# A bias table on POOL's DMA queue, block weights on VectorE, and a longer POOL list at the start of a fused attention and expert kernel

## The chip, the cores and the metric

The kernel runs as one program on one core of a Trainium2 chip. The metric is the device time of one execution in microseconds (us). Before the change the median of three runs is 571.19 us (570.97 to 571.46).

## The reference

Attention with a learned relative bias, then a token and channel mixer, then eight experts of which each token takes one. Only the first part is touched by the change:

```python
B, H, S, D = q.shape                      # 2, 8, 576, 64
scores = scale * np.matmul(q, k.transpose(0, 1, 3, 2))
psi_rel = np.log1p(np.abs(rel))
psi_i = np.log1p(np.maximum(pos[:, None].astype(np.float32), 1.0))
x = (psi_rel / psi_i)[..., None]
h = np.maximum(x @ w1 + b1, 0.0)          # 576 x 576 x 32
bias = h @ w2                             # 576 x 576 x 8
scores = scores + bias.transpose(2, 0, 1)[None, :, :, :]
```

The softmax of the scores, the product with `v`, the mixer and the experts follow.

## The kernel before

The bias is a two-layer network over all pairs of positions, made once per query tile and shared by both batches. It is made in 36 groups of 16 query rows. In one group, 128 partitions hold 4 rows times 32 hidden units, and four parts of 576 columns make 16 rows. The first layer of a group is `bias_hidden` (L484 to L498): each part is one instruction of 128x576, the relu of a table times a scale, on VectorE, POOL (`eng.tensor_scalar`, L497) or ScalarE (L494). It needs the table `tabs`, the scale `sc` and `negb`, the negative of the table `b1c` (`bias_setup`, L463 to L465). The second layer is `bias_mm` (L500): eight matmuls against `wblk`, a 128x32 matrix with the 32x8 weights `w2r` four times on its block diagonal (L196, L197). ScalarE adds a constant `cb` and moves the result out as `ev` (L510), and SP's queue spreads it into the tile's bias (L516 or L518). There are two buffers for a group's first layer, so the first layer of group n+2 waits for the matmuls of group n.

Four of the groups belong to the last query tile, the tail, which is worked first. Before the loop over steps there is a start of hand-written order: `load_const` (L174) issues the loads of the tables and of the first keys and queries, lets TensorE multiply zeros, and builds `wblk`; then `ORDER["start"]` (L58) lists what is emitted on all engines. In that list `hidden0` to `hidden5` and `bias0` to `bias4` are the two layers of the groups, `const` makes `cb` with small matmuls against `wblk` (L479, L481), `zero` clears the query buffers `qt` on POOL (L297, L298), `tail_split` splits the tail's queries in two precisions (`qm`, on POOL, L203 and L305), and `key_T` and `key_split` transpose and split keys (`kn` to `K`; L269, L203, L282). Each engine works off its instructions in this order, and waits by semaphores alone. Which engine takes a part of a first layer is a string in `ENGINE` (L65): the n-th group takes the n-th letter, counted round, so that `start1="VVP"` gives the second part of groups 0 to 4 to V, V, P, V, V (V is VectorE, P is POOL, A is ScalarE).

After the start comes one step per pair of heads and query tile: scores on TensorE (L370), bias and row maximum on VectorE (L348), exponential on ScalarE (L351), and so on. The mixer and the experts are not touched.

Of the kernel before, what the change touches and what calls it, by code (L numbers as in the profile page):

```python
# [54 lines left out]
QO = 3, 3, 3, 6  # L55

ORDER = {
    "start": "hidden0 const load_k2 tail_split0 hidden1 bias0 hidden2 bias1 key_T00 hidden3 zero key_T01 key_T11 key_T10 key_split0 tail_split1 bias2 hidden4 bias3 load_k4 hidden5 key_split1 tail_T bias4 load_v load_q".split(),  # L58
    "first": "scores0 hidden2 last_T prob_T0 values key_T0 normalize query_T tail_T query_split hidden1 hidden0 key_T1 bias_mm key_split out_T tail_split hidden3 query_rest".split(),
    "mixed": "hidden2 scores0 values tail_T query_T normalize hidden0 last_T prob_T0 key_T0 key_T1 query_split tail_split hidden1 key_split bias_mm query_rest out_T hidden3".split(),  # L60
    "bias": "query_T query_split hidden3 scores0 scores1 last_T values hidden0 query_rest hidden2 late bias_mm out_T mix prob_T0 prob_T1 hidden1 normalize".split(),
    "edge": "hidden0 bias_mm mix hidden2 last_T hidden3 prob_T0 scores0 scores1 values query_T prob_T1 normalize query_split query_rest late hidden1 out_T".split(),
    "plain": "scores0 last_T query_T scores1 values normalize prob_T0 prob_T1 out_T query_split query_rest late mix".split(),
}
ENGINE = dict(key0="A", key1="A", keyl0="V", keyl1="A", qlo="P", mhi="P", mlo="P", qhi="AP", qT="A", qT0="V", qT1="AVV", prob0="A", prob1="AV", last="V", half0="V", half1="A", xlo="PPPPVPPVV", val="V", val0="V", hidden0="V", hidden1="VP", hidden2="PV", hidden3="A", early0="V", early1="A", early2="P", early3="A", start0="VA", start1="VVP", start2="V", start3="VA")  # L65

LATE = dict(alloc_mix=9, decode=[10, 12, 14, 16, 17, 20, 22, 24, 26], split_wt2=[-3, -4, 0, -4, 8, 21, 23, 25, 28], split_wt1=[33, 34, 37, 36, 36], split_x=[32, 34, 36, 37, 38, 37, 38, 39])
GATE = -1.7881393e-07
# [40 lines left out]
def body(ctx, tc, q, k, v, w1, b1, w2, wt1, wt2, wc1, wc2, wg, wl, mw1, mw2,  # L109
# [17 lines left out]
    with tc.manual_schedule():  # L127
        tok = ctx.enter_context(ExitStack())
        mix = TokenMix(nc, x)
        attention(tc, nc, tok, mix, q, k, v, w1, b1, w2, c_L, c_id, ident, x, wt1, wt2, prefill)  # L130
        if "x" in dbg:
            nc.sync.dma_start(dbg["x"], x)
        R = Routing(tc, nc, wg, wl, ident, c_tok, c_small, x2d, meta)
        X = Experts(tc, nc, R, Rings(tc, ctx, "big", side="right"), x_p, mw1, mw2, ident, x2d, meta, out)
        mixer(tc, nc, tok, mix, wc1, wc2, ident, x, R, X)
        if "x2" in dbg:
            nc.sync.dma_start(dbg["x2"], x2d)
        X.rest()
        X.close()
        R.close()  # L140


def attention(tc, nc, tok, mix, q, k, v, w1, b1, w2, c_L, c_id, ident, x, wt1, wt2, prefill):
# [10 lines left out]
    with ExitStack() as ctx:  # L154
# [8 lines left out]
        def alloc_ps():  # L163
            return ps_t.tile([128, 512], F32, name="tp", tag="tr")
# [4 lines left out]
        b1c = cst.tile([128, 1], F32, name="b1c")  # L169
        w2r = cst.tile([128, H], F32, name="w2r")  # L170
        wblk = cst.tile([128, 32], F32, name="wblk")

        def load_const():
            four = lambda ap, n: ap.rearrange("(a k) o -> a k o", a=1).to_broadcast([4, HID, n])  # L174

            cut = 4 * NG + S + 128
            warm = cst.tile([128, 1], F32, name="warm")
            nc.vector.memset(warm, 0.0)
            nc.scalar.activation(warm, warm, AF.Exp)
            nc.sync.dma_start(tabs[:, 0:cut], c_L[:, 0:cut])  # L180
            nc.scalar.dma_start(w1c, four(w1.rearrange("o k -> k o"), 1))
            nc.sync.dma_start(b1c, four(b1.rearrange("(k o) -> k o", o=1), 1))
            nc.sync.dma_start(w2r, four(w2, H))
            load_k(0)
            load_q(*steps[0])
            nc.sync.dma_start(tabs[:, cut:], c_L[:, cut:])
            nc.sync.dma_start(ident, c_id)

            zero = x[:, 0]
            nc.vector.memset(zero, 0.0)  # L190
            ps = alloc_ps()
            for _ in range(WARM):
                nc.tensor.matmul(ps, lhsT=zero[:, 0:128], rhs=zero, start=True, stop=True)
            nc.gpsimd.memset(wblk, 0.0)
            for ii in range(4):
                r = slice(32 * ii, 32 * ii + 32)  # L196
                nc.gpsimd.tensor_copy(wblk[r, 8 * ii:8 * ii + 8], w2r[r])  # L197

        turns = {what: cycle(engines) for what, engines in ENGINE.items()}

# [19 lines left out]
        def load_k(i):  # L220

            b, pr = divmod(i, NP)
            n = nat_p.tile([128, 20, D], F32, name="kn", tag="kn", bufs=2)
            main, hs = n[:, 0:16].rearrange("p (n h) d -> p n h d", h=4), k[b, 2 * pr:2 * pr + 4]
            for j in range(NIT):
                nc.sync.dma_start(main[:, j], hs[:, 128 * j:128 * j + 128].rearrange("h p d -> p h d"))
            nc.sync.dma_start(n[0:64, 16:20], hs[:, 512:S].rearrange("h p d -> p h d"))
            for j in range(2):
                nat["k", i + j] = main[:, :, 2 * j:2 * j + 2], n[0:64, 16 + 2 * j:18 + 2 * j]
# [14 lines left out]
        def load_q(it, i):  # L244

            b, pr = divmod(i, NP)
            n = nat_p.tile([128, 4, D], F32, name="qn", tag="qn", bufs=2)
            if it == NIT:
                tv = q[b, :, 512:S].rearrange("(a e) p d -> e p a d", e=2)
                for e in range(2):  # L250
                    nc.sync.dma_start(n[64 * e:64 * e + 64], tv[e])
                for j in range(NP):
                    nat["q", it, i + j] = n[:, j]
            else:
                nc.sync.dma_start(n, q[b, 2 * pr:2 * pr + 4, 128 * it:128 * it + 128].rearrange("h p d -> p h d"))
                nat["q", it, i] = n
# [210 lines left out]
        def hidden_by(g):  # L467

            n = groups.index(g)
            phase = "start" if n < ahead else "early" if n < ahead + B * NP else "hidden"  # L470
            return "".join(e[n % len(e)] for e in (ENGINE[f"{phase}{qq}"] for qq in range(4)))

# [114 lines left out]
        def split_x(n):  # L587
# [3 lines left out]
            else:  # L591
                hl = [kv_p.tile([128, DM], F32R, name="xs", tag=f"K{n - (n > LAST)}{a}") for a in range(2)]
            nc.scalar.copy(hl[0], x[:, n])
            (nc.gpsimd if ENGINE["xlo"][n] == "P" else nc.vector).tensor_tensor(
                hl[1], x[:, n], hl[0].bitcast(F32), ALU.subtract)
# [32 lines left out]
        def late_fetch(s):  # L628

            if pieces and any(f is decode for f, *_ in late.get(s, ())):  # L630
                fetch(pieces.pop(0))

        load_const()
        bias_setup()
        start = {
            "const": (bias_const,), "zero": (query_zero,), "load_k2": (load_k, 2), "load_k4": (load_k, 4), "load_v": (load_v, 0),
            "load_q": (load_q, *steps[NP]), "tail_T": (tail_T, *steps[0]),
        }
        for n in range(2):
# [691 lines left out]
class Experts:  # L1331
# [93 lines left out]
    def weights(self, t, a):  # L1425
        nc, tab = self.nc, self.R.tab
        if t not in self.sel:
            self.sel[t] = (nc.values_load(tab[0:1, 1, t:t + 1], engines=[SP], min_val=0, max_val=E - 1),
                           nc.values_load(tab[0:1, 2, t:t + 1], engines=[SP], min_val=0, max_val=1))
        e, changed = self.sel[t]  # L1430
        self.load(a, e, **(dict(cond=changed) if t > NSAME else {}))
# [359 lines left out]
```

## Time and profile before

| | us |
|---|---|
| median of three runs | 571.19 (570.97 to 571.46) |
| the profiled execution, its own time | 572.25 |
| its span in the trace | 570.1 |
| busy: TensorE, VectorE, ScalarE, POOL | 543.3, 381.8, 331.9, 244.3 |

The profiled execution takes 2.15 us more than its span, and lies 1.06 us above the median of the runs. Times in the trace count from the start of the span. A row of a timeline has the start, the time to the end of the last of its instructions, the engine, the line, the operation, what it writes and reads, how many instructions were merged, and in brackets how long the engine was idle before it and what ended that. Merged instructions of one engine overlap a little, since one starts before the one ahead has written its last value.

### The profile page before, as it was taken

How to read it: one execution, taken by the hardware profiler on the slowest of the kernel's cores; microseconds unless marked ns; L12 is line 12 of the kernel's file. 1: busy time of each engine (PE TensorE's matmuls, PEld its weight loads, DVE VectorE, ACT ScalarE, POOL GpSimd, SP SyncE). 2: the span in 40 equal slices, each digit the busy share in tenths (PEclk: the TensorE clock that was granted, in tenths of full speed). 3: DMA queues.
4: the chain of work that ended last, by engine and by line, in shares of the span. 5: the costliest groups of instructions: out<-in, count | busy, mean ns of one | idle time of the engine just before them, and what ended most of it. 6: DMA issues, size and time to landing. Idle time of an engine off the chain costs nothing.

```text
span 570.1 us, 11965 instructions
## 1 busy us (share of the span) xinstructions
PE 543.3 (95%) x4306; PEld 428.7 (75%) x4306; DVE 381.8 (67%) x886; ACT 331.9 (58%) x622; POOL 244.3 (43%) x236
## 2 busy tenths in 40 slices
PE   8799899999999999999999989999999999999992
PEld 3466677777778977789999867787778778786871
DVE  6788798989987764898888247533681235669640
ACT  5799799899897862444444133123323357776760
POOL 4787656566772540244444102300033145647541
PEclk9999999999999999999999999999999999999997
DMA  6794875765654430344441030270004973566950
GB/s 166 176 199 111 187 172 145 174 148 128 162 131 114 121 102 2 111 121 147 152 161 55 0 93 1 83 268 20 19 20 139 392 272 121 188 251 209 363 168 13
DMA packets 72417, 79.92 MB, mean 140 GB/s; under 512 B 37127, under 2 KB 51725, under 8 KB 72349
## 3 DMA queue, kind: packets, MB, share of 16 engines
q1 hardware_dynamic: 68924, 73.80, 45.0%
q0 software_dynamic: 2176, 5.26, 2.7%
q8 instruction: 36, 0.59, 0.5%
q14 instruction: 33, 0.26, 0.1%
q10 hardware_dynamic: 1248, 0.01, 0.1%
HBM read 72.08 MB, written 5.34 MB: 136 GB/s over the span
## 4 chain that ended last, share of the span: by engine, by line
PE 68%; DVE 12%; ACT 7%; issue 6%; DMA 4%; POOL 1%; SPq 0%; POOLq 0%; ACTq 0%; DVEq 0%
PE ph L770 20%; PE po L770 15%; PE tp L436 5%; PE py L770 5%; PE ps L507 5%; PE ps L370 4%; PE tp L421 3%; ACT t L351 2%; DMA bias<-ev 2%; DVE t L348 2%; DVE K L282 2%; PE tp L770 1%; PE tp L1476 1%; DVE raw L754 1%; DMA raw<-in_moe_w_ch_dram 1%
## 5 line engine op out<-in xcount | busy, mean ns | idle before, releaser
L497 POOL TENSOR_SCALAR hd<-tabs,sc,negb 128x576 f32<-128x576 f32 x32 | 76.6, 2395 | 3.3 <-PE tp L452 1.8
L770 PE MATMUL po<-cw,h 128*128 128x512 f32 x272 | 67.3, 395 | 0.0
L351 ACT ACTIVATE t<-t,st 128x576 f32<-128x576 f32 x72 | 55.4, 770 | 18.4 <-DVE st L348 18.3
L1439 DVE TENSOR_TENSOR big<-raw,big 128x1024 fp32r<-128x1024 f32 x30 | 43.8, 1485 | 21.9 <-ACT big L1438 21.7
L770 PEld LDWEIGHTS po<-cw,h 128*128 128x128 f32 x272 | 49.8, 188 | 10.0 <-issue 0.4
L348 DVE CUSTOM_DVE_ANT_0 t<-ps,bias 128x576 f32<-128x576 f32 x72 | 52.2, 750 | 7.2 <-PE ps L370 4.5
L370 PE MATMUL ps<-K,qt 128*128 128x288 f32 x320 | 54.0, 309 | 2.8 <-DVE qt L209 2.0
L436 PE MATMUL tp<-pt,v 128*64 128x128 f32 (+1 forms) x800 | 49.3, 268 | 0.0
L1217 POOL DMA_INDIRECT meta<-tokid,posi x10 | 10.0, 996 | 90.3 <-DVE tokid L1214 54.4
L370 PEld LDWEIGHTS ps<-K,qt 128*128 128x128 f32 x320 | 44.5, 189 | 5.2 <-POOL t L362 2.1
L770 PE MATMUL py<-big,hT 128*128 128x512 f32 x184 | 47.9, 400 | 0.1
L507 PE MATMUL ps<-hd,wblk 128*32 128x288 f32 x576 | 45.2, 418 | 2.3 <-DVE st L348 1.1
L1438 ACT CAST big<-raw 128x1024 fp32r<-128x1024 f32 x44 | 44.2, 1055 | 2.7 <-DMA big<-in_moe_w_dram 1.0
L436 PEld LDWEIGHTS tp<-pt,v 128*64 128x64 f32 x800 | 40.2, 137 | 7.4 <-issue 5.3
L770 PE MATMUL ph<-big,xT 128*128 128x512 f32 x168 | 43.2, 404 | 1.1 <-DVE xT L1453 1.1
L497 DVE TENSOR_SCALAR hd<-tabs,sc,negb 128x576 f32<-128x576 f32 x69 | 41.8, 636 | 0.1
L762 POOL TENSOR_TENSOR big<-wf,big 128x512 fp32r<-128x512 f32 x12 | 18.7, 1558 | 51.1 <-ACT big L761 51.1
L770 PEld LDWEIGHTS py<-big,hT 128*128 128x128 f32 x184 | 33.8, 188 | 8.2 <-issue 0.6
L494 ACT ACTIVATE hd<-tabs,b1c,sc 128x576 f32<-128x576 f32 x43 | 36.9, 866 | 3.9 <-DVE sc L465 3.8
L1439 POOL TENSOR_TENSOR big<-raw,big 128x1024 fp32r<-128x1024 f32 x10 | 27.5, 2750 | 24.9 <-ACT big L1438 24.9
L770 PEld LDWEIGHTS ph<-big,xT 128*128 128x128 f32 x168 | 30.5, 189 | 10.0 <-issue 1.6
L421 PE MATMUL tp<-ident,t 128*128 128x128 f32 x256 | 34.2, 275 | 0.0
(304 smaller groups left out, 1189.1 us busy)
## 6 DMA issues: line engine op xcount, KB each, us to landing
raw<-in_moe_w_dram SPq DMA_DIRECT2D x48, 512.0 KB
raw<-in_moe_w_ch_dram SPq DMA_DIRECT2D x24, 512.0 KB
bias<-ev SPq DMA_DIRECT2D x32, 288.0 KB
qt<-qs SPq DMA_DIRECT2D x64, 128.0 KB
lw<-in_moe_w_dram SPq DMA_DIRECT2D x16, 512.0 KB
big<-in_moe_w_dram SPq DMA_DIRECT2D x8, 512.0 KB
lw<-in_moe_w_dram SPq DMA_DIRECT2D x16, 256.0 KB
big<-in_moe_w_dram SPq DMA_DIRECT2D x16, 256.0 KB
```

What stands on the lines that cost most here:

```text
L348: nc.vector.tensor_tensor_reduce(t.rearrange("p (a j) -> p a j", a=2), ps[:, :, 0:HALF], bs.rearrange("p (a j) -> p a j", a=2), op0=ALU.ad ...
L351: nc.scalar.activation(t, t, AF.Exp, bias=st[:, j:j + 1], scale=-1.0, accum_out=st[:, 2 + j:3 + j])
L370: nc.tensor.matmul(ps[:, hf, 0:HALF], lhsT=qt[:, j], rhs=K[k][:, hf * HALF:(hf + 1) * HALF], start=j == pairs[0][0], stop=j == pairs[-1][0])
L421: nc.tensor.transpose(tp[:, 128 * j:128 * j + 128], tt[:, o:o + 128], ident)
L436: nc.tensor.matmul(po[64 * h:64 * h + 64, 0:rhs.shape[1]], lhsT=lhsT, rhs=rhs, start=j == 0, stop=j == 4)
L494: nc.scalar.activation(hd[:, qq], Lt[:, o:o + S], AF.Relu, bias=b1c, scale=sc[:, c])
L497: eng.tensor_scalar(hd[:, qq], Lt[:, o:o + S], sc[:, c], negb, ALU.mult, ALU.max)
L507: nc.tensor.matmul(ps[32 * qq:32 * qq + 32, hf, 0:HALF], lhsT=wblk, rhs=hd[:, qq, hf * HALF:(hf + 1) * HALF], start=True, stop=True)
L762: nc.gpsimd.tensor_tensor(lo, src, hi.bitcast(F32), ALU.subtract)
L770: nc.tensor.matmul(out, lhsT=lhs[a], rhs=rhs[b], start=first and i == 0, stop=last and i == 2)
L1438: nc.scalar.copy(hi, raw)
L1439: (nc.gpsimd if c == 3 and t else nc.vector).tensor_tensor(lo, raw, hi.bitcast(F32), ALU.subtract)
```

## The change

Four edits, all at the start. The load of `b1c` is issued on POOL's queue instead of SP's. The four copies that build `wblk` leave `load_const` for a function of their own, run on VectorE, and stand behind `hidden0` in the list. The clearing of the query buffers goes from the middle of the list to its head. And `ENGINE` has `start1="VPPVVP"` where it had `start1="VVP"`, which for the five groups means V, P, P, V, V instead of V, V, P, V, V: one part of `hidden1` goes from VectorE to POOL.

```diff
 ORDER = {
-    "start": "hidden0 const load_k2 tail_split0 hidden1 bias0 hidden2 bias1 key_T00 hidden3 zero key_T01 key_T11 key_T10 key_split0 tail_split1 bias2 hidden4 bias3 load_k4 hidden5 key_split1 tail_T bias4 load_v load_q".split(),
+    "start": "zero hidden0 weights hidden1 const load_k2 tail_split0 bias0 hidden2 bias1 key_T00 hidden3 key_T01 key_T11 key_T10 key_split0 tail_split1 bias2 hidden4 bias3 load_k4 hidden5 key_split1 tail_T bias4 load_v load_q".split(),
...
-            nc.sync.dma_start(b1c, four(b1.rearrange("(k o) -> k o", o=1), 1))
+            nc.gpsimd.dma_start(b1c, four(b1.rearrange("(k o) -> k o", o=1), 1))
             nc.sync.dma_start(w2r, four(w2, H))
...
             nc.gpsimd.memset(wblk, 0.0)
+
+        def weights():
             for ii in range(4):
                 r = slice(32 * ii, 32 * ii + 32)
-                nc.gpsimd.tensor_copy(wblk[r, 8 * ii:8 * ii + 8], w2r[r])
+                nc.vector.tensor_copy(wblk[r, 8 * ii:8 * ii + 8], w2r[r])
...
-            "const": (bias_const,), "zero": (query_zero,), "load_k2": (load_k, 2), "load_k4": (load_k, 4), "load_v": (load_v, 0),
+            "const": (bias_const,), "weights": (weights,), "zero": (query_zero,), "load_k2": (load_k, 2), "load_k4": (load_k, 4), "load_v": (load_v, 0),
```

Lines behind the new function are two higher in the changed kernel (L497 becomes L499). TensorE's and ScalarE's instructions keep their order; SP's list loses one load, its second. The two other lists change as follows.

POOL, from the start of the program's own instructions to the second `qm` pair; before:

```order
L194 MEMSET wblk_103 128x32
L197 COPY wblk_103<-w2r_102 32x8 x4
L203 CAST qm_177<-qn_121 128x2x64
L305 ISA
L305 TENSOR_TENSOR qm_177<-qn_121,qm_177 128x64
L497 TENSOR_SCALAR hd_199<-tabs_99,sc_107,negb_106 128x576
L297 MEMSET qt0_104 128x2x2x64
L298 MEMSET qt0_104 128x2x2x64
L297 MEMSET qt1_105 128x2x2x64
L298 MEMSET qt1_105 128x2x2x64
L203 CAST qm_256<-qn_121 128x2x64
```

The same place on POOL now:

```order
L182 DMA b1c_101<-in_b1_dram 128x1x1
L194 MEMSET wblk_103 128x32
L299 MEMSET qt0_104 128x2x2x64
L300 MEMSET qt0_104 128x2x2x64
L299 MEMSET qt1_105 128x2x2x64
L300 MEMSET qt1_105 128x2x2x64
L499 ISA
L499 TENSOR_SCALAR hd_147<-tabs_99,sc_107,negb_106 128x576
L205 CAST qm_186<-qn_121 128x2x64
L307 TENSOR_TENSOR qm_186<-qn_121,qm_186 128x64
L499 TENSOR_SCALAR hd_203<-tabs_99,sc_107,negb_106 128x576
L205 CAST qm_256<-qn_121 128x2x64
```

`hd_147` is `hidden1`, and `hd_199` before and `hd_203` now are both `hidden2`. The load of `b1c` leads, the four clearings come ahead of all relu parts, a new relu part stands ahead of the first `qm` pair, and the four copies are gone.

VectorE, from the first instruction that reads a loaded table to the first copy of keys; before:

```order
L464 TENSOR_SCALAR negb_106<-b1c_101 128x1
L465 TENSOR_SCALAR sc_107<-tabs_99,w1c_100 128x144
L497 TENSOR_SCALAR hd_138<-tabs_99,sc_107,negb_106 128x576 x4
L481 COPY cb0_148<-tp_143 128x1
L481 COPY cb1_155<-tp_150 128x1
L481 COPY cb2_162<-tp_157 128x1
L481 COPY cb3_169<-tp_164 128x1
L497 TENSOR_SCALAR hd_180<-tabs_99,sc_107,negb_106 128x576 x2
L497 TENSOR_SCALAR hd_199<-tabs_99,sc_107,negb_106 128x576 x3
L497 TENSOR_SCALAR hd_226<-tabs_99,sc_107,negb_106 128x576 x2
```

The same place on VectorE now:

```order
L466 TENSOR_SCALAR negb_106<-b1c_101 128x1
L467 TENSOR_SCALAR sc_107<-tabs_99,w1c_100 128x144
L499 TENSOR_SCALAR hd_138<-tabs_99,sc_107,negb_106 128x576 x4
L199 COPY wblk_103<-w2r_102 32x8 x4
L499 TENSOR_SCALAR hd_147<-tabs_99,sc_107,negb_106 128x576
L483 COPY cb0_157<-tp_152 128x1
L483 COPY cb1_164<-tp_159 128x1
L483 COPY cb2_171<-tp_166 128x1
L483 COPY cb3_178<-tp_173 128x1
L499 TENSOR_SCALAR hd_203<-tabs_99,sc_107,negb_106 128x576 x3
L499 TENSOR_SCALAR hd_230<-tabs_99,sc_107,negb_106 128x576 x2
```

`hd_138` is `hidden0`, `hd_180` before and `hd_147` now are `hidden1`, and the last row is `hidden3`. The four copies of `wblk` stand behind the four parts of `hidden0`; `hidden1` has one part here instead of two, and it comes ahead of the `cb` copies, which wait for TensorE.

## Rows read from the trace of the kernel before

**Rows 1.** The profile's page, the chain that ended last, shares of the span by engine

```profile
PE 68%; DVE 12%; ACT 7%; issue 6%; DMA 4%; POOL 1%; SPq 0%; POOLq 0%; ACTq 0%; DVEq 0%
```

**Rows 2.** The chain from 0 to 20 us in order of time: start, length, what

```profile
1.21 0.75 SPq L182
...
2.01 3.75 DMA w2r<-in_w_dram
...
8.11 2.54 PE ps L507 x32
...
10.67 0.68 ACT ev L510
...
13.44 3.68 DMA bias<-ev
...
17.23 0.75 ACT ev L510
```

**Rows 3.** Timeline of VectorE (DVE) from 0 to 32 us

```profile
5.59 0.15 DVE L464 TENSOR_SCALAR negb<-b1c 128x1 f32<-128x1 f32 x1 [4.15 <-DMA b1c<-in_b_dram]
...
6.01 2.05 DVE L497 TENSOR_SCALAR hd<-tabs,sc,negb 128x576 f32<-128x576 f32 x4
7.99 0.44 DVE L481 COPY cb<-tp 128x1 f32<-128x1 f32 x4
8.34 3.88 DVE L497 TENSOR_SCALAR hd<-tabs,sc,negb 128x576 f32<-128x576 f32 x7
...
14.41 0.46 DVE L282 TENSOR_TENSOR K<-tp,K 64x64 fp32r<-64x64 f32 x2 [0.49 <-ACT K L203]
...
19.70 0.29 DVE L209 TENSOR_SCALAR qt<-tp 128x128 fp32r<-128x128 f32 x1
21.52 0.76 DVE L348 CUSTOM_DVE_ANT_0 t<-ps,bias 128x576 f32<-128x576 f32 x1 [1.53 <-PE ps L370]
...
26.87 0.76 DVE L348 CUSTOM_DVE_ANT_0 t<-ps,bias 128x576 f32<-128x576 f32 x1
```

**Rows 4.** Timeline of POOL from 0 to 32 us

```profile
0.75 0.12 POOL L194 MEMSET wblk<- 128x32 f32 x1 [0.29 <-POOLq L1784]
5.91 1.72 POOL L197 COPY wblk<-w2r 32x8 f32<-32x8 f32 x4 [5.03 <-DMA w2r<-in_w_dram]
9.30 0.29 POOL L203 CAST qm<-qn 128x128 fp32r<-128x128 f32 x1 [1.67 <-DMA qn<-in_q_dram]
...
10.08 2.82 POOL L497 TENSOR_SCALAR hd<-tabs,sc,negb 128x576 f32<-128x576 f32 x1
12.86 0.30 POOL L297 MEMSET qt<- 128x256 f32 x1
```

**Rows 5.** Timeline of all engines, two rows of TensorE (PEld loads weights)

```profile
9.46 0.63 PEld L507 LDWEIGHTS ps<-hd,wblk 128*32 128x32 f32 x12 [0.35 <-DVE hd L497]
...
12.95 2.41 PE L507 MATMUL ps<-hd,wblk 128*32 128x288 f32 x30 [0.21 <-POOL hd L497]
```

**Rows 6.** Line 1217, the only POOL-queue DMAs of 128 small rows: POOL's time, landing

```profile
L1217 POOL DMA_INDIRECT meta<-tokid,posi x10: 928/974/1194, 350.8 to 426.0; - x10
...
DMA to landing us min/median/max: 3.4/3.7/5.5
```

**Rows 7.** DMA queues (q1 is SP's, q10 ScalarE's), 3.5 to 4, then 4 to 4.5 us

```profile
q10 hardware_dynamic: 110, 0.00, 11.6%
...
DMA packets 281, 0.06 MB, mean 121 GB/s; under 512 B 281, under 2 KB 281, under 8 KB 281
...
q1 hardware_dynamic: 281, 0.06, 56.9%
```

**Rows 8.** Relu parts: two of VectorE beside POOL's; all of POOL's to 60 us (ns)

```profile
10.33 1.41 DVE L497 TENSOR_SCALAR hd<-tabs,sc,negb 128x576 f32<-128x576 f32 x2
...
L497 POOL TENSOR_SCALAR hd<-tabs,sc,negb x9: 2280/2286/2918, 10.1 to 53.5; 128x576 f32<-128x576 f32 x9
```

**Rows 9.** Busy time by stretch; the last columns are granted clock, DMA share, GB/s

```profile
26.83:30.25 3.42, 3.42 (x26) 1.94 (x24) 2.82 (x10) 2.61 (x7) 2.12 (x3) 0.50 1.05 216
```

More of the change, by code (lines that the diff above doesn't have):

```diff
@@ L64 @@
 }
-ENGINE = dict(key0="A", key1="A", keyl0="V", keyl1="A", qlo="P", mhi="P", mlo="P", qhi="AP", qT="A", qT0="V", qT1="AVV", prob0="A", prob1="AV", last="V", half0="V", half1="A", xlo="PPPPVPPVV", val="V", val0="V", hidden0="V", hidden1="VP", hidden2="PV", hidden3="A", early0="V", early1="A", early2="P", early3="A", start0="VA", start1="VVP", start2="V", start3="VA")
+ENGINE = dict(key0="A", key1="A", keyl0="V", keyl1="A", qlo="P", mhi="P", mlo="P", qhi="AP", qT="A", qT0="V", qT1="AVV", prob0="A", prob1="AV", last="V", half0="V", half1="A", xlo="PPPPVPPVV", val="V", val0="V", hidden0="V", hidden1="VP", hidden2="PV", hidden3="A", early0="V", early1="A", early2="P", early3="A", start0="VA", start1="VPPVVP", start2="V", start3="VA")
 LATE = dict(alloc_mix=9, decode=[10, 12, 14, 16, 17, 20, 22, 24, 26], split_wt2=[-3, -4, 0, -4, 8, 21, 23, 25, 28], split_wt1=[33, 34, 37, 36, 36], split_x=[32, 34, 36, 37, 38, 37, 38, 39])
```

## The prediction

> **What bounds the kernel now.** I began with the chain on the page [rows 1]: TensorE carries 68% of it, so most of the 571 us is out of this change's reach. All four edits lie in the first 20 us, so I read that stretch alone, first its chain [rows 2]. There the reader sees which load comes last: SP issues `b1c` for 0.75 us, then `w2r` at 2.01; `w2r` lands 3.75 us later; POOL copies it into `wblk` from 5.91 to 7.63 [rows 4]; TensorE makes the constants and then the second layers of groups 0 and 1, which end at 10.65 [rows 2]; ScalarE takes over at 10.67. VectorE's timeline [rows 3] tells almost the same from its side: it waits 4.15 us for `b1c`, starts at 5.59, and until the query tile at 19.70 (ending 19.99) it is idle for only 0.49 us, before 14.41, where it waits for ScalarE. So two chains run side by side. One goes through `w2r` and POOL's copies to TensorE, the other through `b1c` to VectorE, and they meet at ScalarE's first eviction. The first softmax, at 21.52, follows from them, and the next comes 5.35 us later at 26.87 [rows 3]; nothing in these steps waits for an absolute time, so I take it that what the start wins or loses is handed on to the end undiminished.
>
> **The load of b1c.** POOL's first own instruction runs at 0.75 [rows 4], so the load is issued there instead of at 1.21 on SP. The trace has no plain POOL-queue load. The nearest rows are the indirect ones of 128 small rows: 974 ns of POOL, and 3.4, 3.7 or 5.5 us (least, median, most) from issue to landing [rows 6]. From 0.75 this gives 4.15, 4.45 or 6.25. I take the median, since the transfer has as many tiny pieces, and keep 4.15 and 6.25 for the range. Before, `b1c` ended VectorE's wait at 5.59, which is 4.38 after its issue. The next instruction, `sc`, also needs `w1c` and `tabs`. ScalarE's queue, which carries `w1c`, has 110 packets between 3.5 and 4.0 and none in the next half microsecond: all 281 packets there are SP's, and all are under 512 bytes while a row of `tabs` has 3,392 [rows 7]. Both tables are thus through by 4.0; with an estimated 0.4 us for the completion to be seen (bounds 0, and the 1.6 until 5.59, where neither was waited for) they allow 4.4. So `negb` starts at about 4.5, and the first relu part 0.42 later, as before (6.01 less 5.59) [rows 3]: **4.9 instead of 6.01**, a lead of 1.1 us.
>
> **What the lead is spent on.** VectorE's four parts of `hidden0` take 1.98 us to the next instruction (6.01 to 7.99) [rows 3], so they would be through at 6.88. But POOL's new part runs beside them now. Beside the POOL part at 10.08, two VectorE parts in a row took 1.41 us [rows 8] instead of 0.49 + 0.57, so one was 0.35 longer, and POOL's part took 2.82 instead of the usual 2.29 [rows 4, 8]. I add 0.35: 7.23. Only then come the four copies. VectorE has no 32x8 copy in the trace; its four `cb` copies take 0.44 us together [rows 3], POOL's four took 1.72 [rows 4]. I take 0.44, since an engine's fixed cost decides for eight values, and keep 1.72 as the bad end. `wblk` is then whole at **7.67 against 7.63 before**. `w2r` comes no later than this: issued at 1.21 instead of 2.01, with 3.75 us to land as before, it is there at about 5.0. The lead of 1.1 us is gone, because the copies, which ran on an idle POOL beside `hidden0`, now stand behind it.
>
> **What remains.** After `wblk`, TensorE needed 3.02 us to the end of group 1 (7.63 to 10.65) [rows 2, 4]. In it lies a wait of 0.35 us for VectorE's second part of `hidden1` [rows 5]. Now VectorE makes one part, which ends at about 8.2, and POOL the other, which ends at 4.9 + 2.82 = 7.7. Group 1 is wanted only when half of the two groups' matmuls are through, about 9.2. So the 0.35 goes: 7.67 + 3.02 - 0.35 = **10.34 instead of 10.65, a gain of 0.31 us**. What is late next there is `wblk` itself.
>
> **The edits I cost at nothing.** The four clearings are 0.25 us apart and take about 1.0 us; POOL was idle for 5.03 us before the copies [rows 4], and with 0.97 for the load, 0.12 for `wblk` and these it is through by about 2.9. If `b1c` were earlier than 2.9 they would cost; it is not. Their old place, 12.86, becomes free for the second `qm` pair, for which nobody waits then. The first `qm` pair waits for `qn`, whose issue moves up by 0.80 (one load less on SP, 1.21 to 2.01 [rows 2]): from 9.30 to about 8.5, after POOL's new part at 7.7. POOL's part of `hidden2`, 0.78 behind it, may start when group 0 has left its buffer, about 9.3, and ends near 12.1 instead of 12.90, so TensorE's wait at 12.95 [rows 5] goes too. I count nothing for it: ScalarE is behind group 1's eviction then, and the next evictions wait for ScalarE and not for TensorE. The keys, the identity and the second half of `tabs` also come 0.80 sooner, which is more than the 0.31 they have to keep up with. ScalarE's eviction at 17.23 waited for the bias transfer of 3.68 us issued at 13.44 [rows 2]; it moves with the eviction or with SP, so it holds nothing back.
>
> **Sum.** -0.31 us: span 569.8, the profiled execution 571.94 instead of 572.25, and against the runs, whose median stands 1.06 us below that execution, 571.19 - 0.3 = **570.9 us**. About 0.2% (1.1 us) is what a measurement of this kernel can tell from no change, so this is no change.
>
> **A rule weighed.** Beside POOL's two parts in the start, one VectorE part each was 0.35 us longer and POOL's 0.53 to 0.63 [rows 8]. The Trainium skill (SBUF — State Buffer, Who interferes with whom) says that VectorE in its two-port mode and POOL exclude each other for a whole instruction, whoever issues first. By that rule the sum would be as in the fourth rival; rows 8 show a much smaller price.
>
> **The rivals.**
> 1. *The early start counts in full.* If `b1c` is no later than `w1c`, POOL takes nothing from VectorE, and VectorE's list, not `wblk`, bounds the start, then the whole lead of 1.26 us (first part at 4.75) is handed on: 569.9 us. For it speaks that VectorE is idle for only 0.49 us in 14; against it, that `wblk` now stands in that list, and that the next group's first layer must wait for TensorE to free a buffer. 17%.
> 2. *b1c comes late (slower).* POOL's queue lands it after 5.5 us, at 6.25, as the slowest of rows 6. Everything in the start waits for it, one to one: 1.8 us later than I forecast, 571.19 - 0.31 + 1.8 = 572.7. It decides from a landing at about 4.8, from which on the start is later than before. For it speaks the spread of rows 6 and that the load shares the DMA engines with `tabs`; against it, that those slow rows were issued one behind the other, and this load is alone on its queue. 10%.
> 3. *Nothing is handed on.* The gain is eaten where the first steps wait for bias transfers, or ScalarE's list sets the start either way: 571.2. The waits of rows 2 on the bias transfers speak for it. 20%.
> 4. *POOL shuts VectorE out.* Were VectorE held for all of POOL's 2.28 us [rows 8], `hidden0` would end at 9.16, `wblk` at 9.60, and group 1 at 12.25: 1.6 us slower, 572.8. Rows 8 speak against it, since two VectorE parts ran beside POOL's for 1.41 us. 3%.
>
> My forecast, from 0.8 us faster (no 0.35 for POOL, `b1c` at 4.15) to 1.0 us slower (copies as long as on POOL), has the remaining 50%.
>
> **How the numbers follow.** Faster by over 0.2% is rival 1, 0.17; slower are rivals 2 and 4, 0.13; the forecast and rival 3 make 0.70. The range reaches from rival 1's 569.9, rounded down to 569.8, to 572.2, which is the forecast with the dear copies, leaving out the 13% of rivals 2 and 4 and little of rival 1.
>
> **What would show it.** Right: `negb` between 4.3 and 4.8, `wblk` whole between 7.3 and 8.0, no wait of TensorE's weight loads for VectorE between groups 0 and 1, ScalarE's eviction of group 1 at 10.2 to 10.6, the first softmax near 21.2. Rival 1 shows a first softmax near 20.3, rival 2 a `negb` near 6, rival 4 a relu part of VectorE of over 2 us. The forecast is wrong altogether if the granted clock changes its place: TensorE has 0.50 of its clock, 1.2 GHz, from 26.83 to 30.25 and is busy all that time [rows 9], some microseconds after it had waited for the query tile that VectorE wrote at 19.70; there the steps hide it, since softmaxes stay 5.35 us apart [rows 3], but under the second layers of the start it would double 2.5 us of matmuls. I see no edit that does this, as the zeros that TensorE multiplies first are untouched.

## The result, and the profile after

| | before | after |
|---|---|---|
| median of 7 runs, us | 571.19 (570.87 to 572.92) | 574.62 (573.72 to 576.27) |
| ratio | | 1.0059 (95%: 1.0043 to 1.0075) |
| the profiled execution and its span | 572.25, 570.1 | 575.66, 573.7 |

The kernel became 0.6% slower: 3.7 us above the forecast and outside its range. The timeline of all engines of the changed kernel has every step of the start:

```profile
1.31 0.91 POOL L182 DMA_DIRECT2D b1c<-in_b_dram  x1 [0.85 <-POOLq L1786]
...
1.50 5.27 PE L193 MATMUL tp<-x 128*128 128x512 f32 x6 [1.50 <-DVE x L190]
...
6.21 0.15 DVE L466 TENSOR_SCALAR negb<-b1c 128x1 f32<-128x1 f32 x1 [4.76 <-DMA b1c<-in_b_dram]
...
6.63 2.48 DVE L499 TENSOR_SCALAR hd<-tabs,sc,negb 128x576 f32<-128x576 f32 x4
6.71 2.93 POOL L499 TENSOR_SCALAR hd<-tabs,sc,negb 128x576 f32<-128x576 f32 x1 [3.35 <-DVE sc L467]
...
9.03 1.30 DVE L199 COPY wblk<-w2r 32x8 f32<-32x8 f32 x4
...
10.47 0.18 PE L481 MATMUL tp<-x,wblk 128*32 128x1 f32 x1 [3.70 <-DVE wblk L199]
...
10.88 4.08 PE L509 MATMUL ps<-hd,wblk 128*32 128x288 f32 x32
...
26.20 0.76 DVE L350 CUSTOM_DVE_ANT_0 t<-ps,bias 128x576 f32<-128x576 f32 x1 [1.48 <-PE ps L372]
...
565.20 0.97 POOL L1497 DMA_INDIRECT out_dram<-y,mt  x1 [0.91 <-ACT y L1496]
```

Read it from the top. POOL issues the load of `b1c` at 1.31, and VectorE waits for it to 6.21, where it had waited to 5.59 [rows 3]. The four parts of `hidden0` end at 9.11, beside POOL's new part, which ends at 9.64. Only then do the copies get through: `wblk` is whole at 10.33, where POOL had it whole at 7.63 [rows 4]. TensorE, whose zeros ended at 6.77, stands for 3.70 us. The 32 matmuls of groups 0 and 1 then take 4.08 us, and the first softmax comes at 26.20 instead of 21.52 [rows 3], **4.68 us later**. Before, the row of the 32 matmuls was

```profile
7.96 2.67 PE L507 MATMUL ps<-hd,wblk 128*32 128x288 f32 x32
```

The chain that ended last, after the change, in order of time (start, length, what):

```profile
1.31 4.88 DMA b1c<-in_b_dram
...
7.12 1.98 DVE hd L499 x3
9.11 0.55 DVE wblk L199
9.67 0.24 DVE wblk L199
9.93 0.16 DVE wblk L199
10.10 0.23 DVE wblk L199
...
10.47 0.61 PE tp L481 x27
11.08 3.89 PE ps L509 x32
14.97 1.05 PE tp L271 x4
```

Group 1 ends at 14.97, 4.64 us behind `wblk`; before, it was 3.00 (7.63 to 10.63; the prediction has 3.02, from the chain). The reason is in the busy time by stretch (columns as in rows 9: TensorE's matmuls first, the granted clock third from the end), first before, then twice after:

```profile
6.40:9.80 3.40, 2.45 (x61) 1.38 (x62) 3.40 (x11) 1.72 (x3) 1.56 (x5) 1.00 0.72 176
...
6.42:9.83 3.41, 0.35 (x1) 0.00 (x0) 3.36 (x7) 1.62 (x2) 3.12 (x2) 1.00 0.71 166
9.83:16.66 6.83, 6.19 (x72) 3.36 (x73) 4.86 (x15) 2.08 (x4) 3.77 (x5) 0.50 0.57 134
```

After the change TensorE is busy for 0.35 us from 6.42 to 9.83, where it was busy for 2.45 before (6.40 to 9.80); in the next stretch, where its work begins, it has half its clock, 1.2 GHz. Before, the trace records no such stretch ahead of the one at 26.83 [rows 9].

How much of this reaches the end? In the trace of before, the last issue of an output row is

```profile
560.60 0.97 POOL L1495 DMA_INDIRECT out_dram<-y,mt  x1 [0.91 <-ACT y L1494]
```

and after it is at 565.20 (above): 4.60 of the 4.68 us are still there. The span grew by 3.6 only, since from that issue to the end it is 9.5 us before and 8.5 after. Two executions far above all others (609.90 us of the kernel before, 1327.66 us of e3) are left out of every ratio; the other executions of the kernel before lie between 569.64 and 574.62 over all comparisons, so in what follows the first softmax of each trace is the measure, and the time the check on it.

### The profile page after: what moved, and what is told of

Its sections match the earlier page's. It is cut to its first block, busy times and chain, and to the rows that moved or that the text cites. A ratio compares the mean times of both kernels' runs of the same rounds, so it can differ in the third digit from the quotient of the medians.

```text
span 573.7 us, 11968 instructions
## 1 busy us (share of the span) xinstructions
PE 544.3 (95%) x4306; PEld 429.1 (75%) x4306; DVE 379.9 (66%) x889; ACT 331.8 (58%) x622; POOL 246.6 (43%) x234
## 4 chain that ended last, share of the span: by engine, by line
PE 66%; DVE 14%; ACT 7%; issue 5%; DMA 4%; POOL 2%; SPq 1%; POOLq 0%; ACTq 0%; DVEq 0%
PE ph L772 20%; PE po L772 15%; PE ps L509 5%; PE py L772 5%; PE tp L438 5%; PE ps L372 4%; PE tp L423 3%; ACT t L353 3%; DVE t L350 2%; DVE hd L499 2%; DVE K L284 2%; PE tp L772 1%; DMA bias<-ev 1%; DMA lw<-in_moe_w_dram 1%; PE tp L1478 1%
## 5 line engine op out<-in xcount | busy, mean ns | idle before, releaser
L499 POOL TENSOR_SCALAR hd<-tabs,sc,negb 128x576 f32<-128x576 f32 x33 | 79.1, 2400 | 12.2 <-DVE hd L499 3.5
L1441 DVE TENSOR_TENSOR big<-raw,big 128x1024 fp32r<-128x1024 f32 x30 | 40.1, 1358 | 25.7 <-ACT big L1440 21.7
L372 PE MATMUL ps<-K,qt 128*128 128x288 f32 x320 | 53.9, 308 | 2.4 <-DVE qt L211 2.0
L372 PEld LDWEIGHTS ps<-K,qt 128*128 128x128 f32 x320 | 44.5, 189 | 4.6 <-issue 2.7
L499 DVE TENSOR_SCALAR hd<-tabs,sc,negb 128x576 f32<-128x576 f32 x68 | 42.4, 650 | 2.0 <-PE ps L509 1.8
```

The costliest lines, as they stand in the source:

```text
L372: nc.tensor.matmul(ps[:, hf, 0:HALF], lhsT=qt[:, j], rhs=K[k][:, hf * HALF:(hf + 1) * HALF], start=j == pairs[0][0], stop=j == pairs[-1][0])
L499: eng.tensor_scalar(hd[:, qq], Lt[:, o:o + S], sc[:, c], negb, ALU.mult, ALU.max)
L1441: (nc.gpsimd if c == 3 and t else nc.vector).tensor_tensor(lo, raw, hi.bitcast(F32), ALU.subtract)
```

## The experiments

Two theories stood against each other. **The clock theory**: the late `wblk` leaves TensorE without work, and the half clock that follows takes about half of the loss. **The parts theory**: the loss is the sum of late pieces (`b1c`, copies, POOL's part), and the clock only goes with them. All in one table; "clock" is where the first half-clock stretch after the zeros begins, if it begins ahead of the first softmax:

| kernel | `negb` | `wblk` whole | group 1 ends | first softmax | clock | ratio of time to before (95%) |
|---|---|---|---|---|---|---|
| before | 5.59 | 7.63 | 10.63 | 21.52 | none | 1 |
| after | 6.21 | 10.33 | 14.97 | 26.20 | 9.83 | 1.0059 (1.0043 to 1.0075) |
| e1, `b1c` on SP | 5.59 | 9.58 | 14.22 | 25.46 | 8.72 | 1.0055 (1.0029 to 1.0081) |
| e2, copies on POOL | 6.12 | 5.64 | 11.18 | 22.02 | none | 0.9996 (0.9984 to 1.0008) |
| e3, part on VectorE | 6.09 | 9.16 | 13.79 | 25.04 | 8.53 | 1.0041 (1.0019 to 1.0062) |
| e4, seven zeros | 6.25 | 10.36 | 12.91 | 24.08 | none | 1.0029 (1.0013 to 1.0046) |
| f1, before, `b1c` on POOL | 6.19 | 8.22 | 11.24 | 22.10 | none | 0.9999 (0.9977 to 1.0020) |
| f2, before, copies moved | 5.58 | 8.65 | 12.81 | 24.52 | 8.78 | 1.0035 (1.0017 to 1.0053) |
| g1, copies ahead | 6.24 | 7.59 | 12.19 | 23.35 | none | 1.0021 (1.0003 to 1.0038) |
| g2, `b1c` on ScalarE's queue | 6.08 | 5.50 | 11.13 | 21.97 | none | 0.9990 (0.9973 to 1.0008) |
| k1, before, one zero | 5.64 | 7.68 | 12.22 | 23.68 | see k1 | 1.0022 (1.0007 to 1.0037) |

Each time on the left is from one trace, but the mean granted clock is on record for every execution. Its median is 0.992 for the kernel before and 0.989 after; it is 0.988 to 0.989 in e1, e3 and f2, and 0.992 or more in e2, e4, f1, g1 and g2. So the fall is not a matter of the traced executions alone. (In h2, below, where the half clock lasts half as long, it is 0.992 too, and k1's half clock is not in the record.)

**e1: `b1c` back on SP.**

```diff
-            nc.gpsimd.dma_start(b1c, ...
+            nc.sync.dma_start(b1c, ...
```

> The changed kernel with b1c loaded on SP's queue again, the other three edits kept. Parts theory (each edit costs its own delay of wblk, and the delay is handed on): negb returns from 6.21 to about 5.6, wblk from 10.33 to about 9.7, first softmax from 26.20 to about 25.6, time about 574.0 us. Clock theory (TensorE, without work from 6.77 to 10.47, loses its full clock, and half the loss is slow matmuls): TensorE still waits about 3 us for wblk; if the granted clock still falls to 0.50 at 9.83, the same 574.0; if it does not, about 572.5 and group 1's matmuls in about 2.4 us instead of 4.08.

```profile
5.59 0.15 DVE L466 TENSOR_SCALAR negb<-b1c 128x1 f32<-128x1 f32 x1 [4.15 <-DMA b1c<-in_b_dram]
...
8.41 1.16 DVE L199 COPY wblk<-w2r 32x8 f32<-32x8 f32 x4
```

`negb` is back at 5.59 and everything behind it comes 0.74 earlier, but the clock still falls. With a falling clock both theories say this, so e1 does not separate them; it shows that the late `b1c` is a small part of the loss.

**e2: the copies back on POOL**, all else as changed.

```diff
-                nc.vector.tensor_copy(wblk[...
+                nc.gpsimd.tensor_copy(wblk[...
```

> The changed kernel with the four copies of wblk on POOL again, ahead of POOL's new relu part; the other three edits kept. Parts theory: w2r has landed by 6.2, POOL's copies end near 7.9, 2.4 us earlier than now, VectorE loses 1.3 us of copies, first softmax near 23.8, time about 572.2. Clock theory: TensorE waits about 1 us for wblk as before the change, the granted clock stays at 1.00 through the start, the whole loss but b1c's 0.6 us goes: first softmax near 22.2, about 571.3.

Timeline of POOL, then two rows of TensorE:

```profile
4.78 0.86 POOL L199 COPY wblk<-w2r 32x8 f32<-32x8 f32 x4 [1.43 <-DMA w2r<-in_w_dram]
...
6.70 3.25 POOL L499 TENSOR_SCALAR hd<-tabs,sc,negb 128x576 f32<-128x576 f32 x1 [1.06 <-issue]
7.18 1.16 PE L509 MATMUL ps<-hd,wblk 128*32 128x288 f32 x4 [0.61 <-DVE hd L499]
...
8.51 2.67 PE L509 MATMUL ps<-hd,wblk 128*32 128x288 f32 x28 [0.16 <-DVE hd L499]
```

`w2r` does land before 5 us, as the prediction had it, and an idle POOL has `wblk` whole at 5.64, before VectorE has its first relu part. No half clock is left in the start, and with it 4.18 of the 4.68 us are gone; the first softmax, 22.02, is near the clock theory's 22.2 and not the parts theory's 23.8, and the time is that of before. Of the four edits this one decides.

**e3: the relu part back on VectorE.**

```diff
-start1="VPPVVP"
+start1="VVP"
```

> The changed kernel with the part of hidden1 back on VectorE (start1 as before), so POOL has nothing beside VectorE's four parts and four copies. Parts theory: no VectorE part and no copy waits for POOL, hidden0 ends 0.4 us earlier and the copies take 0.4 instead of 1.3 us: wblk at about 9.1 instead of 10.33, group 1 then waits for the second part, first softmax near 25.2, time about 573.6. Clock theory: TensorE waits 2.3 us; the clock falls or not; if it stays at 1.00, first softmax near 23.6 and about 572.0.

```profile
6.51 2.05 DVE L499 TENSOR_SCALAR hd<-tabs,sc,negb 128x576 f32<-128x576 f32 x4
8.47 0.68 DVE L199 COPY wblk<-w2r 32x8 f32<-32x8 f32 x4
```

Without POOL beside them the four parts take 2.05 and not 2.48 us, and the copies 0.68 and not 1.30. With `negb` 0.12 earlier, that is the 1.16 us that the first softmax gains, as the parts theory has it. The clock still falls.

**e4: seven zero matmuls instead of three**, so that TensorE works on until just before `wblk`; every other edit stays.

```diff
-WARM = 3
+WARM = 7
```

> The changed kernel with seven zero matmuls at the start instead of three, so that TensorE works until about 10.3 and hardly waits for wblk; nothing else moves. Clock theory: the granted clock stays at 1.00, groups 0 and 1 take 2.4 instead of 4.08 us, the transposes of the keys 0.3 us less, first softmax near 24.2, time about 572.7. Parts theory (the clock is beside the point): first softmax stays at 26.2, time 574.6 or a little more.

```profile
6.42:9.83 3.41, 3.40 (x8) 1.14 (x6) 3.36 (x7) 1.63 (x2) 3.08 (x2) 1.00 0.65 159
9.83:16.66 6.83, 6.06 (x100) 3.51 (x104) 5.97 (x17) 4.38 (x8) 4.11 (x5) 1.00 0.67 160
```

`wblk` is as late as after the change (10.36), and TensorE is busy all through the first stretch. It keeps its clock, 1.00 where it was 0.50, and from `wblk` to the end of group 1 takes 2.55 instead of 4.64 us. The first softmax gains 2.12, near the clock theory's 24.2, and the median time, 573.19, is 1.4 us lower. Nothing else was touched, so this is the price of the clock alone; against the parts theory, the loss is more than its pieces.

**f1 and f2: one edit alone, on the kernel before.** f1 moves the load of `b1c` to POOL's queue; f2 moves the copies to VectorE, behind `hidden0`.

> The kernel before with one edit alone: b1c loaded on POOL's queue. Parts theory as the first four runs leave it (b1c itself costs 0.6 to 0.7 us, because POOL issues it at about 1.3 and one DMA engine lands its share late): negb at 6.1 to 6.25 instead of 5.59, granted clock 1.00 through the start, first softmax 21.5 + 0.6 = 22.1, time +0.6 us. Rival (POOL's queue is as good as SP's when nothing else is moved, so w2r, which is issued 0.8 us earlier, wins): wblk whole by about 7.0, first softmax near 21.2, time -0.3 us.

> The kernel before with one edit alone: the four copies of wblk on VectorE behind the four parts of hidden0. No POOL part stands beside them. Clock theory: wblk whole at 8.4 to 8.5 instead of 7.63, TensorE waits about 1.7 us from 6.77; the granted clock falls if that wait is already too long (it fell at 2.4 us of wait in the run with the part back on VectorE), then group 1 ends near 12.7 and the first softmax is near 24; if it does not fall, group 1 ends near 11.2 and the first softmax is near 22.1. Parts theory: 22.3 in any case.

f1, timeline:

```profile
6.19 0.15 DVE L464 TENSOR_SCALAR negb<-b1c 128x1 f32<-128x1 f32 x1 [4.75 <-DMA b1c<-in_b_dram]
...
8.55 2.70 PE L507 MATMUL ps<-hd,wblk 128*32 128x288 f32 x32
```

f2, busy time by stretch:

```profile
8.78:12.19 3.41, 3.39 (x60) 2.03 (x64) 2.39 (x8) 0.74 (x1) 1.29 (x3) 0.50 0.90 219
```

`b1c` alone makes the start 0.58 later and leaves the clock in this trace, and no difference in the time can be told. (The ten executions of f1 fall in two groups, four from 569.95 to 570.22 and six from 572.11 to 573.37. The trace is of the first group; what the second did is not shown.) The copies alone make the start 3.00 later: `wblk` is only 1.02 later than before, but the clock halves, and from `wblk` on another 1.2 us go to group 1 (4.16 instead of 3.00). The remaining 0.8 us come with a second half-clock stretch, from 22.43 to 25.84: the eight score matmuls of the first step (L370 before, L372 here) take 2.16 us instead of 1.35.

f2 also shows what the length of TensorE's wait hangs on. Its zeros ended at 6.24 and not at 6.74, with the granted clock on record at 1.00 from 5.36 on and not from 6.35, so TensorE stood for 2.55 us and not for the 1.7 expected. (e3 is alike: it stood for 3.18 us there, and not for the 2.4 that the expectation of f2 reads off.) The moments at which the clock rises and falls differ from trace to trace (the record of 1.00 starts between 5.06 in h2 and 6.90 in h1, leaving out k1), so one trace does not say that a wait of this length always costs the clock. Nine of f2's ten executions have a mean granted clock of 0.987 to 0.990; the tenth, at 0.994, is the fastest, 571.71 us.

**g1 and g2: could the change be mended?** g1 puts the copies ahead of `hidden0` on VectorE. g2 is e2 with `b1c` on ScalarE's queue.

```diff
-    "start": "zero hidden0 weights hidden1 ...
+    "start": "zero weights hidden0 hidden1 ...
```

> The changed kernel with the copies on VectorE ahead of hidden0 instead of behind it; the rest as changed. Order theory (VectorE is not too slow for the copies, they stand in the wrong place): w2r is there at about 5 to 6.2, so wblk is whole by 6.6 to 6.9, TensorE waits for hidden0 alone, the clock stays at 1.00, first softmax between 22.0 and 22.6, time 571.2 to 571.8. Engine theory (VectorE's copies are dear wherever they stand, 1.3 us): hidden0 starts 1.3 us later, first softmax near 23.5, time 572.8.

> The changed kernel with b1c loaded on ScalarE's queue behind w1c, and the copies of wblk on POOL; the early clearing and POOL's new part kept. If b1c is what bounds the start once wblk is early: negb at 4.5 to 5.0, hidden0 done by 7.4, groups 0 and 1 from about 7.0 to 9.8, first softmax near 20.7, time about 570.4, faster than both kernels. Rival (b1c lands no sooner, since its tiny pieces share the DMA engines with tabs and the keys): negb at 5.6 or later, first softmax 21.5 to 22, time 571.2 to 571.7.

g1, timelines of VectorE and of POOL:

```profile
6.54 1.05 DVE L199 COPY wblk<-w2r 32x8 f32<-32x8 f32 x4
7.63 2.88 DVE L499 TENSOR_SCALAR hd<-tabs,sc,negb 128x576 f32<-128x576 f32 x5
...
6.74 2.48 POOL L499 TENSOR_SCALAR hd<-tabs,sc,negb 128x576 f32<-128x576 f32 x1 [3.38 <-DVE sc L467]
```

g2, timeline of VectorE:

```profile
6.08 0.15 DVE L466 TENSOR_SCALAR negb<-b1c 128x1 f32<-128x1 f32 x1 [4.63 <-DMA b1c<-in_b_dram]
```

g1 keeps the clock and saves 2.85 of the 4.68, but the copies now push the relu parts to 7.63, and the first softmax, 23.35, is near the 23.5 of the engine theory. g2 equals e2, and `b1c` comes at 6.08, no sooner than from POOL's queue (6.09 in e3), though it is issued at 2.11 and not at 1.31. The rival in its expectation holds.

**k1: the clock by itself**, on the kernel before: one zero matmul instead of three, no part of the change.

> The kernel before with one zero matmul at the start instead of three; no other instruction moves, so negb, wblk and hidden0 keep their times (5.59, 7.63, 8.07). Clock theory, tested without any part of the change: TensorE has worked too little when wblk comes, groups 0 and 1 run at a granted clock of 0.50 and take about 4.1 us instead of 2.7, the key transposes 0.3 us more: group 1 ends near 12.1 instead of 10.63, first softmax 23.2 to 23.6, time +1.8 us. Rival (the matmuls were slow in the changed kernel for another reason, such as their operands coming late): first softmax stays at 21.5.

```profile
1.50 2.07 PE L193 MATMUL tp<-x 128*128 128x512 f32 x2 [1.50 <-DVE x L190]
...
8.18 4.05 PE L507 MATMUL ps<-hd,wblk 128*32 128x288 f32 x32
```

`wblk` is as early as before (7.68), but TensorE stands from 3.57, and the 32 matmuls take 4.05 us, as after the change. The profile has no record of the clock there until 13.51, so the durations must speak. In e4 they tell what no record means: the weight loads of the zeros come 0.85 us apart up to 5.07, ahead of its first record at 5.66, and 0.43 apart from 5.80 on, at 1.00. So the zeros run at half clock at first. In k1 the clock had not yet risen when the 32 matmuls ran, where in the changed kernel it had risen and fell again; the price is the same. k1's first softmax is 2.16 later, and its time 0.2% longer (1.0022), a little less than expected. e4 takes 2.12 off the changed kernel and k1 adds 2.16 to the one before; the two agree.

**h1 to h3: can `b1c` come sooner from SP?** h1, on the kernel before, issues it ahead of `tabs`; h2 issues `b1c` and `w2r` ahead of `tabs`; h3 is e2 with `b1c` first on SP.

> The kernel before with b1c issued first on SP's queue, then tabs, then w2r. If b1c is late because its tiny pieces come behind tabs and beside the keys on the DMA engines, and not because of its queue: negb near 3, the scale waits for tabs, which comes 0.8 us later than before, at about 4.8; hidden0 starts near 5.2 instead of 6.01, wblk whole by about 7.0, first softmax near 20.8, time -0.7 us. Rival (the keys behind now hold up w2r and the end is the same): first softmax 21.3 to 21.6, time the same.

> The kernel before with b1c and w2r issued ahead of tabs on SP's queue. wblk is then whole early, by about 5; tabs comes 1.3 us later than before, at about 5.3, and becomes what VectorE waits for: hidden0 starts near 5.7, group 0 right behind its parts, first softmax near 21.1, time -0.4 us. Rival: tabs is later still, because two transfers of tiny pieces are ahead of it on the same DMA engines, hidden0 at 6.0 or later, no gain.

> The changed kernel with b1c issued first on SP's queue and the copies of wblk on POOL, the early clearing and POOL's new part kept. If the two dear parts of the change are the queue of b1c and the engine and place of the copies, this keeps only the harmless half: hidden0 near 5.2, wblk by 6.5, clock 1.00, first softmax 20.8 to 21.2, time -0.4 to -0.7 us. Rival (POOL's new part, which waits for the copies and then runs beside VectorE, holds up group 1): first softmax 21.5 or later, later than with b1c first alone by 0.5 us or more.

h1, timeline:

```profile
4.25 0.15 DVE L464 TENSOR_SCALAR negb<-b1c 128x1 f32<-128x1 f32 x1 [2.81 <-DMA b1c<-in_b_dram]
...
7.63 0.29 DVE L465 TENSOR_SCALAR sc<-tabs,w1c 128x144 f32<-128x144 f32 x1 [3.22 <-DMA w1c<-in_w_dram]
7.91 1.67 POOL L197 COPY wblk<-w2r 32x8 f32<-32x8 f32 x4 [7.03 <-DMA w2r<-in_w_dram]
```

h2, timeline of VectorE:

```profile
7.32 0.29 DVE L465 TENSOR_SCALAR sc<-tabs,w1c 128x144 f32<-128x144 f32 x1 [3.17 <-DMA tabs<-in_c_L_dram]
```

All three miss. `b1c` comes 1.3 to 1.6 us sooner (`negb` at 4.25, 4.00 and 4.19), but `sc` then waits for the other loads, to 7.63, 7.32 and 7.88, and TensorE with it. In h1 the last of them is `w1c`, though ScalarE issued it at 0.92 as before. The first softmax comes at 25.70, 24.04 and 26.07, with half-clock stretches from 10.31, 8.47 and 8.73, and the ratios are 1.0055 (1.0037 to 1.0073), 1.0025 (1.0010 to 1.0040) and 1.0066 (1.0043 to 1.0089). No version here beats the kernel before.

**What the runs settle.** Of the 4.68 us at the first softmax, the half clock takes about 2.1 (e4, k1), and the late `wblk`, with the pieces that make it late, the rest. In that rest POOL's part is 1.16 (e3) and `b1c` 0.5 to 0.7 (f1, what e2 leaves, e1); by subtraction about 0.8 is left for the copies' place in VectorE's list. These are not independent: with the copies on POOL (e2) all goes but 0.50.

## Why the prediction was wrong, point by point

**"The load of b1c": mis-sized.** I had it issued at 0.75 and landing at 4.45, the median of [rows 6]. It was issued at 1.31, 0.56 later than POOL's first own instruction before, and took 4.88 us, between the median and the most of those rows. Of the sixteen signals of its landing (semaphore updates) in the trace, twelve came by 4.68 and the last at 6.18: most of it was there about when I had it, and `negb` waited for the rest. The tables, which I had through by 4.0, were: their last signal before is at 4.00. `negb` came at 6.21 instead of about 4.5: 1.71 us. The second rival had this (6.25) and gave 10% to it; but against SP's queue, from which `negb` ran at 5.59, f1 prices it at 0.58 us, a small part of the loss. I also credited the lead to the queue. Issued by SP, ScalarE and POOL, the load released `negb` at 5.58 to 5.64, 6.08 and 6.09 to 6.25 (e1, g2, and the others): another issuing engine wins nothing. The Trainium skill (DMA: Bandwidth & Descriptors, Issuing engines are not separate DMA queues) says that loads from any engine run on the same 16 DMA engines and that only the time of issuing is saved. The runs fit it in that no queue landed the load sooner than SP's, and here not even the time of issuing was won; which DMA engines carried the load no run here shows.

**"What the lead is spent on": right in kind, the copies mis-sized.** `hidden0` took 2.40 us (6.63 to 9.03), where I had 2.33 with 0.35 for POOL's part beside it. The copies took 1.30, where I had taken 0.44 from the `cb` copies [rows 3] and kept 1.72 as the bad end. Alone on VectorE they take 0.68 (e3). The rest goes with POOL's part: the first copy, due at 9.11, ended at 9.66, just after POOL's part ended at 9.64. I had priced POOL's part beside the relu parts and forgot that the copies would stand beside it too. The fourth rival, that POOL shuts VectorE out, does not hold for the parts: the first two took 1.50 us together beside POOL, by their row of VectorE's timeline, one longer by about as much as in [rows 8]. That one copy looks like it, but in g1 the copies are through at 7.59 beside a part of POOL that runs from 6.74 to 9.21. The Trainium skill (SBUF — State Buffer, Who interferes with whom) has an exclusive lock for both while VectorE is in its two-port mode. The one copy would agree with it; if the parts and g1's copies are in that mode, they don't. Why that copy was held stays open. `wblk`: 1.71 + 0.07 + 0.86 = 2.64 of the 2.66 us by which 10.33 missed the forecast 7.67.

**"What remains": the step that failed.** From `wblk` to the end of group 1 I had 3.02 - 0.35 = 2.67 us. It took 4.64. The wait of 0.35 [rows 5] did go: the 32 matmuls ran without a break, and at full clock (e4) the stretch took 2.55. But it ran at half clock. I had named this case in "What would show it", with its price (it "would double 2.5 us of matmuls"), and dismissed it: "I see no edit that does this, as the zeros that TensorE multiplies first are untouched." The zeros were untouched, but the work behind them was moved: TensorE's next instruction waits for `wblk`, and I had put `wblk` at the same time as before. The two errors are one chain. With `wblk` at 7.63 (before) and 7.59 (g1) the clock held, so at my 7.67 it probably would have; at 10.33 it did not. I ought to have asked what a late `wblk` does to TensorE's idle time, and to have priced the second rival with it: its 572.7 us has the delay one to one and no clock.

**"The edits I cost at nothing": right.** The clearings were through by 3.4 us, and POOL was idle for 3.35 us before its part, as the bracket of its row shows. TensorE's wait for POOL's part of `hidden2` [rows 5] is gone; in its place its weight loads wait 0.46 and 0.61 us for ScalarE's parts, from 17.71 on, later than all that is told here.

**Handing on: right for this change, too strict as a rule.** 4.68 us at the first softmax are 4.60 at the last issue, so rival 3 falls. But "undiminished" does not hold for every kernel here: e4 gains 2.12 us on the changed kernel at the first softmax and 4.16 at the last issue, and f1 turns a loss of 0.58 into a gain of 1.12 (see the last point below).

**The signs.** Slower had 13%, by two mechanisms that both occurred in part (`b1c` late, POOL against VectorE). Neither alone explains 0.6%; the edit that costs most is one that I had priced at 0.44 us, the copies in VectorE's list (f2: 3.00 us alone), and the fall of the clock, which I had named as a sign, had no chance of its own.

## What to carry to other kernels

When a small operation moves from an idle engine to a busy one, look for whoever waits longest behind it. If that is TensorE at the start of a stretch of matmuls, the delay can be paid twice, as here: once as the wait, and once more at half clock. Read the granted clock of that stretch in the trace. Judge a change at the start by the first step that all later work follows from (here the first softmax) and not by the total, whose spread is as large as the effect.

## What the runs showed of the hardware that was not expected

- The same 32 matmuls took 2.67 us before (f1: 2.70) when TensorE had been busy shortly before, and 4.08 (k1: 4.05) after it had stood for 3.70 us (k1: 4.15). Four more zero matmuls, which compute nothing, made the changed kernel's start 2.12 us faster.
- POOL issued its first load 0.56 us later than it had run its first own instruction, and the load's row is 0.91 us long; its landing took 4.88 us.
- Small loads ahead of `tabs` on SP's queue delayed the tables: `sc` ran at 7.32 to 7.88 instead of 5.68, where it had not waited for them. In h1 the last signal of `tabs` came at 7.26 instead of 4.00, and `w1c` on ScalarE's queue was late too. Why small loads hold the others up that long is open; no run separates it.
- Open, too, is a difference of 1 to 1.7 us that arises between about 515 and 530 us, in the experts, among kernels with the same code there (f1 is 0.54 us behind the kernel before until 515 us and 1.12 ahead at the last issue, 559.48), and the 8.5 to 9.6 us behind the last issue. They blur the times, not the first softmax by which the runs are judged here.
